# One transfer for each store, and a plan that overlaps operations of ScalarE and VectorE

## The chip, the cores and the metric

The kernel runs on one core of one Trainium2 chip. A core has a matrix engine (TensorE, PE in the profile; PEld is its weight load), a vector engine (VectorE, DVE), a scalar engine (ScalarE, ACT), GpSimd (POOL) and SyncE (SP), which here does nothing but issue transfers. Each engine works through its own list of instructions and waits on semaphores for the others. Sixteen DMA engines move data between DRAM and the on-chip memory. The metric is the time of the whole program on the device, in microseconds; smaller is better.

## The reference

Two mixers over a sequence of S = 2048 positions and D = 640 channels, and a gate that blends them:

```python
kv = k_shift * v                       # k_shift: 4-tap causal shift convolution of k
y  = irfft(rfft(kv) * rfft(ssm_k))     # causal convolution of length 2048 per channel
a  = q * (y + kv * ssm_D)
b  = attention(q @ wqkv) @ wo          # 32 heads of 20, window of 8 keys, dilation 2
g  = sigmoid((q * gate_w).sum(-1, keepdims=True))
out = g * a + (1 - g) * b              # [1, 2048, 640] bf16
```

Here q is `A_q`, which is also the input of the attention.

## The kernel before

**The plan.** The kernel is written as some 25 generators (`vproj`, `score_gen`, `u_stream`, `mults`, ...). Each yields a request `Req`: which engine, a cost in ns, which events must have happened, how many PSUM slots it takes (there are four) or gives back. `Plan.run` keeps, for every engine, the time `self.at[e]` at which it is free, takes in turn the request with the smallest start plus a priority, and lets the generator emit its instructions. So the order of every engine's list, and the choice between ScalarE ("A") and VectorE ("D") where a request allows both ("AD"), follow from these modelled times. On the chip the lists run in that order, and semaphores alone decide when.

**The stages.** `transposes` brings `A_q` into `xT`; `qkproj` (L596) and `vproj` (L534) project; `score_gen` (L662), exponentials (L670) and `pv_gen` (L696) do the attention; VectorE does the shift convolution beside it (L474, L489, L491). The long convolution is a two-step transform: first-stage units of 8 matmuls (`s1_unit`, L729) and second-stage units of 32 (`s2_unit`, L747), first for the filter (`h_stream`), then for kv (`u_stream`), in five groups of 16 channels; each unit's PSUM result is cast by ScalarE (L271) or VectorE (L273). VectorE multiplies the transforms group by group (`mults`, L866 and L869: eight instructions of 128 x 1024 a group). `inverse1` (L883, four units a group) and `inverse2` (L960) go back; `outproj` (L999) makes the attention's output, scaled by 1 - g (L1010) and reordered by GpSimd's transfers into `bl` (L1019).

**The end of the kernel.** `load_q` fetches `A_q` again into `qg`, which takes over the buffer of `kv` (tag "kv"), in 16 transfers of 160 KB; `qscale` (L937, 16 instructions) multiplies `qg` by the gate. For every group of three columns t, `inverse2` makes y in PSUM, ScalarE copies it (L969), VectorE multiplies it into `qg` (L972). `adds` (L1027) adds `bl` to two columns t - 1 and t at a time, and calls `store(t)`.

**The rows.** Partition 32 gg + i of `qg` holds, at column t, the output row 64 i + 16 gg + t. So a pair of columns is, per partition, 2 x 640 values that lie next to each other in the output (2560 bytes), with a step of 64 rows between partitions of a group gg and of 16 rows between the four groups. Before, `store` issues one transfer per group gg, of 32 partitions; for t = 1 and 5 it stores nothing, and at t = 3 and 7 four columns at once. That makes 24 transfers: 20 from SyncE, two from GpSimd (t = 3), two from ScalarE (t = 15).

The load is planned so (L915): a request to GpSimd waits for the last first-stage matmul on kv, and the requests to SyncE that follow it name no event:

```python
yield Req("G", 1.0, [ev("us1")])
...
r = yield Req("S", 900.0, move=us(327680, 1280) * 1.5)
```

Of the kernel before, what the change touches and what calls it, by code (L numbers as in the profile page):

```python
# [18 lines left out]
D = 640  # L19
# [123 lines left out]
LAT = {("P", "A"): 230.0, ("P", "D"): 230.0, ("A", "P"): 120.0, ("D", "P"): 120.0, ("A", "D"): 100.0, ("D", "A"): 100.0}  # L143


MODE = dict(score_gen=1, h_stream=2, u_stream=2, inverse2=4)


class Plan:
# [45 lines left out]
    def best(self, r, name=""):  # L195
        if r.engs == "P":
            st = self.start(r, "P")
            if st == INF:
                return INF, INF, "P"
            st += 110.0 if MODE.get(name) != self.mode else 0.0  # L200
            return self.fetch(st, self.cost(r, "P") * (2.0 if st < 7500.0 else 1.0), r.ins), st, "P"
        return min((self.start(r, e) + self.cost(r, e) + (r.lean if e == "A" else 0.0), self.start(r, e), e) for e in r.engs)

    def run(self):
        while self.streams:
            pick = None
            for k, (pri, gen, r) in enumerate(self.streams):
                end, st, e = self.best(r, gen.__name__)
                if st == INF:
                    continue  # L210
                p = pri if r.pri is None else r.pri
                key = (st + 120.0 * p, p, k)
                if pick is None or key < pick[0]:
                    pick = (key, k, st, end, e)
            assert pick is not None, [s[2].engs for s in self.streams]
            _, k, st, end, e = pick
            pri, gen, r = self.streams[k]
            end -= r.lean if e == "A" else 0.0
            g = Grant()
            g.eng, g.banks = e, []  # L220
            if e == "P":
                self.mode = MODE.get(gen.__name__)
                self.fetch(st, end - st, r.ins, True)
            g.done = Ev(end, e)
            self.at[e] = end
            if r.move:
                at = max(self.pipe, st + 1300.0)
                self.pipe = at + r.move
                g.done = Ev(self.pipe + 700.0, "X")
                self.lane[e].append(g.done.t)  # L230
            if r.take:
                for s in sorted(self.slots, key=lambda s: INF if s.free.t is None else s.free.t)[:r.take]:
                    s.free = Ev(None)
                    g.banks.append(self.slots.index(s))
            for s in r.give:
                self.slots[s].free = Ev(end, e)
            try:
                self.streams[k][2] = gen.send(g)
            except StopIteration:
                del self.streams[k]  # L240
# [3 lines left out]
def kernel(  # L244
# [14 lines left out]
    nc = tc.nc  # L259
# [6 lines left out]
    def raw(ap, off, dims):  # L266
        return bass.AP(tensor=ap.tensor, offset=ap.offset + off, ap=dims)
# [77 lines left out]
    def us(nbytes, run):  # L345
        return 1.1 * nbytes / 16.0 / run * (10.0 + run / 24.0)
# [3 lines left out]
    def loads():  # L350
        def load(name, dst, src, nb, run, deps=()):
            g = yield Req("S", 300.0 + nb / run * 0.5, deps, move=us(nb, run))
            nc.sync.dma_start(dst, src)
            mark(name, g)
# [71 lines left out]
    st = {}  # L426
# [550 lines left out]
                mark(f"pr{t}", e)  # L977

    def store(t):
        if t in (1, 5):  # L980
            return
        t0 = t - 3 if t < 8 else t - 1
        for gg in range(4):
            eng = nc.gpsimd if t < 4 and gg % 2 else nc.scalar if t == 15 and gg % 2 else nc.sync
            eng.dma_start(raw(outf, (16 * gg + t0) * D, [[64 * D, 32], [1, (t - t0 + 1) * D]]),
                          st["qg"][32 * gg:32 * gg + 32, t0:t + 1, :].rearrange("p t c -> p (t c)"))

    def outproj():
        yield Req("G", 1.0, [ev("oT"), ev("wo"), ev("gate")])
# [33 lines left out]
    def adds():  # L1023
        for t in range(1, 16, 2):
            yield Req("D", 740.0, [ev(f"bl{t}"), ev(f"pr{t}")])
            qg, bl = st["qg"], st["bl"]
            nc.vector.tensor_tensor(qg[:, t - 1:t + 1, :], qg[:, t - 1:t + 1, :], bl[:, t - 1:t + 1, :], ALU.add)  # L1027
            store(t)
# [68 lines left out]
```

## Time and profile before

| | before |
|---|---|
| time, median of 3 runs | 251.08 us (249.28 to 254.05) |
| profiled execution: span | 248.4 us |
| TensorE busy | 211.4 us, 85% |
| VectorE busy | 178.4 us, 72% |
| ScalarE busy | 182.5 us, 73% |
| GpSimd busy | 67.7 us, 27% |
| moved by DMA | 42.67 MB, 172 GB/s on average |
| stores of the output to landing | 1.8 us (80 KB), 2.7 us (160 KB) from SyncE |

A busy share is an average over stages that have different limits, so it doesn't tell what a change in one stage is worth. The stages are read from tables of windows, and the order of events in one stage from the timeline. The time to landing of a transfer runs from its issue until its data are there. The profile's span leaves out a small part of the device time.

### The profile page before, as it was taken

How to read it: one execution, taken by the hardware profiler on the slowest of the kernel's cores; microseconds unless marked ns; L12 is line 12 of the kernel's file. 1: busy time of each engine (PE TensorE's matmuls, PEld its weight loads, DVE VectorE, ACT ScalarE, POOL GpSimd, SP SyncE). 2: the span in 40 equal slices, each digit the busy share in tenths (PEclk: the TensorE clock that was granted, in tenths of full speed). 3: DMA queues.
4: the chain of work that ended last, by engine and by line, in shares of the span. 5: the costliest groups of instructions: out<-in, count | busy, mean ns of one | idle time of the engine just before them, and what ended most of it. 6: DMA issues, size and time to landing. Idle time of an engine off the chain costs nothing.

```text
span 248.4 us, 9692 instructions
## 1 busy us (share of the span) xinstructions
PE 211.4 (85%) x4294; PEld 160.9 (65%) x4294; DVE 178.4 (72%) x225; ACT 182.5 (73%) x218; POOL 67.7 (27%) x137
## 2 busy tenths in 40 slices
PE   7999989999999998888889569899979999995400
PEld 3765635655455666566769468889969999994300
DVE  0666879999999644578687667979597639946850
ACT  3437587767787799989998656689797978986810
POOL 7803703664251246340000000033030333033100
PEclk9999999999999999955556979999999999999555
DMA  6997499966697373898994856791140119951464
GB/s 185 354 338 272 114 312 349 280 145 180 109 184 156 96 185 83 196 233 152 284 326 86 197 109 149 159 217 58 57 172 3 55 40 227 205 121 55 137 175 116
DMA packets 51753, 42.67 MB, mean 172 GB/s; under 512 B 27280, under 2 KB 46864, under 8 KB 51712
## 3 DMA queue, kind: packets, MB, share of 16 engines
q1 hardware_dynamic: 46928, 32.87, 52.1%
q0 software_dynamic: 4688, 9.03, 14.1%
q8 instruction: 33, 0.54, 1.0%
q10 hardware_dynamic: 96, 0.16, 0.3%
q14 instruction: 8, 0.07, 0.1%
HBM read 23.51 MB, written 5.25 MB: 116 GB/s over the span
## 4 chain that ended last, share of the span: by engine, by line
PE 49%; DVE 18%; ACT 10%; issue 8%; DMA 7%; SPq 2%; POOL 1%; DVEq 0%; ACTq 0%
PE pj L596 11%; PE op L999 7%; PE i L883 7%; PE psv L534 6%; ACT ET L670 6%; PE s L747 5%; PE O L696 4%; DVE pb L474 4%; DVE pa L489 3%; PE s L729 3%; PE sc L662 3%; DMA qg<-in_A_q_dram 2%; DMA Wv<-in_B_wqkv_dram 2%; DVE Hb L273 2%; SPq L923 2%
## 5 line engine op out<-in xcount | busy, mean ns | idle before, releaser
L670 ACT ACTIVATE ET<-sc 128x726 bf16<-128x726 f32 (+1 forms) x80 | 64.5, 864 | 5.1 <-PE sc L662 4.7
L596 PE MATMUL pj<-xT,Wqk 128*128 128x363 bf16 (+3 forms) x250 | 48.4, 343 | 1.8 <-DVE oS L710 1.2
L596 PEld LDWEIGHTS <-Wqk 128*128 128x128 bf16 x250 | 23.0, 97 | 20.5 <-DVE oS L710 1.9
L747 PE MATMUL s<-Am,Gs 64*128 64x64 bf16 x1280 | 29.7, 201 | 6.4 <-issue 4.1
L747 PEld LDWEIGHTS <-Gs 64*128 64x128 bf16 x1280 | 26.5, 102 | 10.2 <-issue 9.0
L273 DVE CAST Am<-s 128x1024 bf16<-128x1024 f32 x20 | 23.9, 1219 | 6.3 <-PE s L729 6.3
L534 PE MATMUL psv<-Wv,xT 128*128 128x320 bf16 x170 | 25.2, 299 | 1.1 <-DMA Wv<-in_B_wqkv_dram 0.5
L999 PE MATMUL op<-wo,Hb 128*128 128x320 bf16 x160 | 25.1, 304 | 0.0
L883 PE MATMUL i<-M,X 128*128 128x128 bf16 x160 | 21.3, 227 | 0.5 <-DVE X L869 0.5
L271 ACT CAST Am<-s 128x1024 bf16<-128x1024 f32 x20 | 20.0, 1030 | 2.4 <-PE s L729 2.2
L271 ACT CAST X<-i 128x1024 bf16<-128x1024 f32 x19 | 19.1, 1012 | 3.4 <-PE i L883 2.3
L1019 POOL DMA_DIRECT2D bl<-X x12 | 6.3, 532 | 56.0 <-ACT X L1010 56.0
L999 PEld LDWEIGHTS <-Hb 128*128 128x128 bf16 x160 | 20.8, 146 | 0.7
L883 PEld LDWEIGHTS <-X 128*128 128x128 bf16 x160 | 20.4, 149 | 0.9 <-DVE X L869 0.9
L534 PEld LDWEIGHTS <-xT 128*128 128x128 bf16 x170 | 16.0, 98 | 7.6 <-issue 1.0
L662 PE MATMUL sc<-qb,kb 31*128 31x121 bf16 x544 | 18.6, 245 | 2.3 <-DVE oS L710 1.0
L1019 POOL DMA_DIRECT2D bl<-room x20 | 10.4, 526 | 33.9 <-ACT room L1010 33.9
L696 PEld LDWEIGHTS <-ET 128*128 128x128 bf16 x544 | 16.1, 100 | 5.1 <-issue 2.7
L696 PE MATMUL O<-VW,ET 128*128 128x21 bf16 x544 | 16.6, 176 | 2.5 <-ACT ET L670 1.5
L662 PEld LDWEIGHTS <-kb 31*128 31x128 bf16 x544 | 10.3, 103 | 12.1 <-issue 8.5
L489 DVE TENSOR_TENSOR pa<-pa,pb 128x2560 bf16<-128x2560 bf16 x12 | 17.9, 1489 | 0.3
L883 PE MATMUL i<-M,Hs 128*128 128x128 bf16 x128 | 17.1, 228 | 0.4 <-ACT X L271 0.4
(83 smaller groups left out, 380.1 us busy)
## 6 DMA issues: line engine op xcount, KB each, us to landing
X<-Hs SPq DMA_DIRECT2D x16, 256.0 KB, 5.6
Hb<-in_A_k_dram SPq DMA_DIRECT2D x4, 640.0 KB, 10.7
kv<-in_A_v_dram SPq DMA_DIRECT2D x4, 640.0 KB, 12.2
kv_scr<-Hb SPq DMA_DIRECT2D x8, 320.0 KB, 5.2
Hb<-in_A_ssm_k_dram SPq DMA_DIRECT2D x16, 160.0 KB, 5.3
kv<-kv_scr SPq DMA_DIRECT2D x8, 320.0 KB, 5.2
qg<-in_A_q_dram SPq DMA_DIRECT2D x16, 160.0 KB, 6.5
Gs<-cf_G SPq DMA_DIRECT2D x8, 256.0 KB, 7.3
```

Of the source, the lines that this page charges most:

```text
L271: nc.scalar.copy(dst, src)
L273: nc.vector.tensor_copy(dst, src)
L489: nc.vector.tensor_tensor(pa[:], pa[:], pb[:], ALU.add)
L534: nc.tensor.matmul(ps[:, bb, 0:320], lhsT=xT[:, dt, BP * (b0 + bb):BP * (b0 + bb) + 128], rhs=Wv[:, dt, c0:c0 + 320], start=(dt == 0), sto ...
L596: nc.tensor.matmul(ps[:, i, 0:n], lhsT=Wqk[:, dt, w, 128 * ft:128 * ft + 128], rhs=rhs, start=(dt == 0), stop=(dt == NDT - 1))
L662: nc.tensor.matmul(scs[h4 // 2][:, h4 % 2, BP * bb:BP * bb + BP], lhsT=kb[r:r + DH + NF, 128 * b:128 * b + 128], rhs=qb[r:r + DH + NF, BP ...
L670: nc.scalar.activation(ETs[e][:, :, 0:nw], scs[hf][:, :, 0:nw], ACT.Exp, scale=SCALE)
L696: nc.tensor.matmul(O[:, o0:o0 + 21], lhsT=ET[:, hh, BP * bb:BP * bb + 128], rhs=VW[:, b, 4 * t + h4, :], start=True, stop=True, skip_group ...
L747: nc.tensor.matmul(o, lhsT=G[rows, j, rr, :], rhs=Am[rows, 2 * j + rr, :, :], start=(rr == 0), stop=(rr == 1), tile_position=(64 * c, 0), ...
L883: nc.tensor.matmul(o, lhsT=src[:, c, :, :, 8 * oc + il].rearrange("p q j -> p (q j)"), rhs=M[:, k, :], start=(k == 0), stop=(k == 1), skip ...
L999: nc.tensor.matmul(op[:, k, 0:320], lhsT=raw(a, HS * (t % 2) + t // 2, [a.ap[0], [8, 128]]), rhs=wo[:, ft, 320 * k:320 * k + 320], start=( ...
L1019: nc.gpsimd.dma_start(bl[32 * gg:32 * gg + 32, t - 1:t + 1, :].rearrange("p t c -> p (t c)"), raw(row, 0, [[4 * pitch, 32], [1, 1280]]))
```

## The change

Two edits. A store becomes one transfer of all 128 partitions, issued by SyncE, every second column: eight transfers of 320 KB. The four groups gg are now the outermost dimension of the pattern on the side of the DRAM (4 x 32 x 1280). And the plan frees ScalarE 130 ns and VectorE 60 ns before the modelled end of an operation (if it is longer than twice that), since the next operation on these engines starts before the last one has ended. It is for better modelled times, and through them for another order of instructions and another choice between the two engines; it adds and removes no computation.

```diff
+HEAD = dict(A=130.0, D=60.0)
...
             g.done = Ev(end, e)
             self.at[e] = end
+            if end - st > 2.0 * HEAD.get(e, 0.0):
+                self.at[e] -= HEAD.get(e, 0.0)
...
     def store(t):
-        if t in (1, 5):
-            return
-        t0 = t - 3 if t < 8 else t - 1
-        for gg in range(4):
-            eng = nc.gpsimd if t < 4 and gg % 2 else nc.scalar if t == 15 and gg % 2 else nc.sync
-            eng.dma_start(raw(outf, (16 * gg + t0) * D, [[64 * D, 32], [1, (t - t0 + 1) * D]]),
-                          st["qg"][32 * gg:32 * gg + 32, t0:t + 1, :].rearrange("p t c -> p (t c)"))
+        t0 = t - 1
+        nc.sync.dma_start(raw(outf, t0 * D, [[16 * D, 4], [64 * D, 32], [1, (t - t0 + 1) * D]]),
+                          st["qg"][:, t0:t + 1, :].rearrange("p t c -> p (t c)"))
```

In the built program, seen engine by engine, the plan's new times move many instructions. TensorE, VectorE, ScalarE and GpSimd keep their work but for the stores and a few casts: net, five casts of 1024 columns go from VectorE to ScalarE. In VectorE's list the 16 `qscale` instructions stood behind the multiplications of all five groups; in the changed list they stand behind those of the third group, ahead of the last two. Of the 16 output projections ten stood ahead of the last first-stage matmul on kv in TensorE's list, and now eight do.

## The prediction

> **What bounds the kernel now.** I read the share of each engine by stage first, then the timeline of the last 50 us, then the waits of SyncE. The stages (columns: stretch in us, its length, busy us and count of PE, PEld, DVE, ACT, POOL, granted clock, DMA share, GB/s):
>
> ```profile
> 150.00:180.00 30.00, 28.94 (x707) 26.91 (x705) 22.94 (x25) 22.95 (x24) 4.22 (x8) 1.00 0.55 125
> ...
> 203.36:221.97 18.61, 18.26 (x352) 17.18 (x350) 15.06 (x30) 15.91 (x18) 5.43 (x11) 1.00 0.94 196
> 221.97:239.43 17.46, 7.68 (x522) 5.97 (x522) 14.36 (x26) 11.16 (x14) 3.11 (x6) 0.76 0.41 117
> 239.43:248.40 8.97, 0.00 (x0) 0.00 (x0) 0.00 (x1) 0.00 (x0) 0.00 (x0) 0.50 0.45 109
> ```
>
> Up to 221.97 TensorE is the bound (97 to 98% busy), then VectorE (82%), and for the last 8.97 us no engine computes: only stores run. The timeline around the load of `qg`, and then at the end (start, length, engine, line, operation, out<-in, and in brackets the idle time before it and what ended that):
>
> ```profile
> 202.81 0.51 PE L729 MATMUL s<-F1b,kv 64*128 64x128 bf16 x8
> ...
> 203.36 10.22 SPq L923 DMA_DIRECT2D qg<-in_A_q_dram  x16
> ...
> 205.29 0.68 DVE L866 TENSOR_TENSOR Hs<-X,Hs 128x1024 bf16<-128x1024 bf16 x1
> ```
>
> ```profile
> 220.63 0.39 DVE L937 TENSOR_SCALAR qg<-qg,g_nat 128x640 bf16<-128x640 bf16 x1 [3.26 <-issue]
> ...
> 221.32 2.16 DVE L937 TENSOR_SCALAR qg<-qg,g_nat 128x640 bf16<-128x640 bf16 x7 [0.29 <-DMA qg<-in_A_q_dram]
> ...
> 221.90 1.02 PE L960 MATMUL i<-X,T 32*32 32x160 bf16 x96
> ...
> 229.30 16.02 SPq L985 DMA_DIRECT2D out_dram<-qg  x20
> ...
> 237.88 1.55 DVE L1027 TENSOR_TENSOR qg<-qg,bl 128x1280 bf16<-128x1280 bf16 x2
> ```
>
> Two things are to be seen. The load of `qg` begins when the last first-stage matmul on `kv` (L729) ends, because it takes that buffer, and its last piece is there only at 221.32, 17.96 us later. VectorE waits for it 3.26 us, but all its multiplications (L866, L869) are behind it by then, and TensorE never notices. And the last add ends at 239.43, while SyncE is still issuing stores until 245.32, about 0.45 us each, after a pause in its wait list:
>
> ```profile
> SPq L985 <- DMA out_dram<-qg: 2.4, 1, 2.4
> ```
>
> **What the Trainium skill says.** (1) "DMA: Bandwidth & Descriptors", section "Why a DMA increments its semaphore by 16 and not by 1": a transfer is spread over k of the 16 engines, the largest k up to 16 that divides the size of the slowest dimension, not 1, of both access patterns. No transfer of SyncE in the trace of before has such a dimension under 16, so it neither agrees nor disagrees. (2) The same page, "Issuing engines are not separate DMA queues": issuing from several engines saves issue time alone. The trace fits: an 80 KB store takes 1.8 us to landing from SyncE and from ScalarE alike. (3) "Perfetto Trace Analysis", "Tensor Engine Instruction": VectorE and ScalarE take their instructions strictly in order. The wait of 3.26 us above, with nothing passing it, agrees. (4) "TensorE: Matmul & The Clock Gate", Part 1: after some 3.4 us of idleness the clock halves. The trace agrees: 32 L747 matmuls take 1.03 us at 113.25 (stage at 0.74) and 0.57 at 202.41 (stage at 1.00).
>
> **The change part by part.**
>
> *Fewer stores.* 24 transfers of 80 or 160 KB (20 from SyncE, 2 from GpSimd, 2 from ScalarE) become 8 of 320 KB from SyncE. Issue falls from 20 x 0.45 us to 8 x 0.45, so the issue queue behind the last add goes away. If each store ran on 16 engines, the end would be: 0.1 us wait, 1.6 us fixed (the 1.8 us to landing less 0.2 us of moving), the last two stores' data (0.9 us each at the rate below), and the 1.7 us that lie now between the last landing (244.89 + 1.8) and 248.4: 5.2 us instead of 8.97, a gain of 3.8.
>
> *The shape of a store.* The new DRAM pattern is 4 x 32 x 1280, so by (1) k is 4: each of four engines carries 327,680 / 4 = 81,920 B per store, and all eight stores want the same four. The rate of one engine I take from the transfers of SyncE in 124 to 130 us, most of them with the same rows of 2560 B; the other two lines bound it: the stores themselves at 242.5 to 245, and long rows at 18 to 24. Columns: packets, MB, share of 16 engines.
>
> ```profile
> q1 hardware_dynamic: 1175, 2.03, 94.9%
> ```
>
> ```profile
> q1 hardware_dynamic: 259, 0.44, 73.3%
> ```
>
> ```profile
> q1 hardware_dynamic: 618, 1.63, 71.7%
> ```
>
> 2.03 MB / (0.949 x 16 x 6 us) = 22.3 GB/s; the stores give 0.44 / (0.733 x 16 x 2.5) = 15.0, the long rows 1.63 / (0.717 x 16 x 6) = 23.7. So a store takes 3.7 us (3.5 to 5.5), eight 29.4 us (27.7 to 43.7). The adds that release them follow each other within some 13 us, so the stores queue and the end is first add + 0.1 + 1.6 + 29.4 + 1.7 = first add + 32.8.
>
> *The plan.* HEAD lets the planner start the next ScalarE or VectorE operation 130 or 60 ns early. That is about what the trace shows (ScalarE casts of 1.01 us start 0.9 apart, L866/L869 of 0.68 start 0.60 apart), but costs nothing itself: it only moves work. In the built order five casts of 1024 columns, net, go over from VectorE to ScalarE; up to the last L729 TensorE's work differs by two output projections only (of 16, ten stood ahead of that matmul, now eight). The earlier stages I book at nothing, within 3 us either way: TensorE has the same instructions and is the bound there, and the row of casts beside it has room (ScalarE 77 to 86% busy in 150 to 203).
>
> What I do book is VectorE's tail. In the built order of before the 16 `qscale` instructions (L937) stand behind all multiplications. In the changed order they stand **ahead of the multiplications of the last two groups**. The planner believes `qg` to be there earlier than it is: `load_q` waits for the last L729 with a GpSimd request, but its eight SyncE requests carry no dependency. Queued behind the first waiting `qscale`: 8 multiplications of group 3, a cast, 8 of group 4. Waiting for those: ScalarE's evictions of group 4 (they overwrite what the multiplications read), so all four PSUM slots, so TensorE, which runs dry about 5 us after the last L729. From that matmul's end, t0:
> - t0: 203.35 less two output projections of 1.4 us = 200.5.
> - `qg` landed: 17.96, less the 8 of 12 `bl` transfers that can't run in the jam. GpSimd's queue took 19.2% of the engines over 19 us for 12, so 8 are 2.4 us: t0 + 15.5.
> - the last seven `qscale`, 0.3 each: 17.7. Multiplications of group 3, 8 x 0.60: 22.5.
> - TensorE: four inverse units (L883) at 1.0 and two projections at 1.4, 0.2 of wait: 29.5. Its clock will be down; half speed for some 4 us costs 2: 31.5.
> - s2 unit 0.6, wait 0.2, VectorE's cast 1.2: 33.5. Multiplications of group 4: 38.3. (Four projections, 5.6 us, lie beside them.)
> - four inverse units and a wait 4.3, last eviction 1.4: 44.0.
>
> So the second inverse (L960) starts at 244.5 instead of 221.97, 22.5 us later. The first add ends 4.4 us after that start (221.97 to 226.37 now): 248.9.
>
> *Sum.* 248.9 + 32.8 = 281.7 us of span against 248.4: +33.3. With 251.08 us before: **284.4**.
>
> **The rivals.**
> - *Jam, but stores on all engines.* For it: nothing in this trace shows a narrow transfer. Last add at 244.5 + 17.5 - 1.5 (no projection lies between any more) = 260.5, + 5.2 = 265.7; +17.3: 268.4.
> - *Narrow stores, no jam.* For it: the 3.26 us wait cost nothing before. Against: the order. 226.4 + 32.8 = 259.2; +10.8: 261.9.
> - *Neither, faster than before.* The issue queue shrinks as meant, 3.8 us: 247.3. Against it stand both arguments.
> - *Slower stores still*, at 15.0 GB/s: +14.3 on the forecast, 298.7. It's the top of the forecast's own case.
>
> **How the numbers follow.** The forecast's case 0.82; it spans 277 (clock penalty 2.0, rate 1.7 and earlier stages 3 us better) to 299 (the slow rate); jam alone 0.09, narrow stores alone 0.05, neither 0.04. Of the first I leave out the top; with the second that makes 8 in 10 for 267 to 297. Faster by over 2% is half of the last case, within 2% the other half and a little.
>
> **What would show it.** Right: VectorE idle 12 us or more ahead of L937, TensorE idle beside it; L866 of group 3 only after L937; stores landing 5 us after issue and later ones 15 to 20; the last landing 20 us or more behind the last add; a DMA share near 0.25 with all four engines busy. Wrong: DMA share over 0.5 while stores run alone (k is 16), or the second inverse starting before 230 (no jam).

## The result, and the profile after

| | before | after |
|---|---|---|
| time, median of 4 runs | 251.87 us (249.28 to 254.05) | 282.97 us (281.35 to 286.37) |
| ratio to before, 95% interval | | 1.125 (1.110 to 1.140) |
| profiled execution: span | 248.4 us | 281.4 us |
| TensorE / VectorE / ScalarE busy | 211.4 / 178.4 / 182.5 us | 215.8 / 171.5 / 185.7 us |
| granted clock of TensorE, mean | 0.896 | 0.845 |

Here and below the medians are of all runs, while the ratios compare only the fast ones, since some executions of one and the same kernel take 1.5 to 3% longer than its others.

The engines do almost the same work, and most of the 33.0 us that the span has grown by are waiting. (In the traces six casts of 128 x 1024, net, have moved from VectorE to ScalarE, 39 and 66 before and 33 and 72 after, where the built order had been read as five.) Two stretches hold the waiting. Both are in the windows of the changed kernel (columns as before: stretch in us, its length, busy us and count of PE, PEld, DVE, ACT, POOL, granted clock, DMA share, GB/s):

```profile
200.00:205.00 5.00, 4.24 (x84) 3.72 (x84) 0.00 (x0) 1.12 (x2) 1.68 (x4) 1.00 1.06 219
205.00:210.00 5.00, 0.00 (x0) 0.00 (x0) 0.39 (x1) 0.00 (x0) 0.00 (x0) 0.79 1.09 196
210.00:215.00 5.00, 0.00 (x0) 0.00 (x0) 2.16 (x7) 0.00 (x0) 0.00 (x0) 0.50 0.98 174
215.00:220.00 5.00, 0.00 (x0) 0.00 (x0) 4.25 (x11) 0.11 (x1) 0.00 (x0) 0.50 0.01 2
220.00:225.00 5.00, 3.19 (x50) 2.85 (x50) 3.12 (x6) 4.11 (x5) 1.50 (x3) 0.50 0.05 18
225.00:230.00 5.00, 5.00 (x44) 4.27 (x43) 0.00 (x0) 2.82 (x3) 0.58 (x2) 0.66 0.13 49
...
260.00:265.00 5.00, 0.00 (x0) 0.00 (x0) 0.00 (x0) 0.00 (x0) 0.00 (x0) 0.50 0.26 102
265.00:270.00 5.00, 0.00 (x0) 0.00 (x0) 0.00 (x0) 0.00 (x0) 0.00 (x0) 0.50 0.26 104
270.00:275.00 5.00, 0.00 (x0) 0.00 (x0) 0.00 (x0) 0.00 (x0) 0.00 (x0) 0.50 0.26 103
```

From 205 to 220 TensorE and ScalarE, which before were busy for 14.65 and 13.23 us of these 15, do next to nothing; until 215 the DMA engines are full (shares of 0.98 to 1.09), and from then to 220 VectorE works almost alone. From 260 on nothing computes and the share of the DMA engines stands at 0.26, steady to the last digit: of 16 engines, four. The records of the single packets (a packet is one row of 2560 bytes) say so too: from 260 to 270 four of them are under way at 87% of the time and five at the rest, never fewer and never more. The timeline says who waits. VectorE's, and then SyncE's (start, length, engine, line, operation, out<-in, and in brackets the idle time before it and what ended that):

```profile
208.60 0.39 DVE L942 TENSOR_SCALAR qg<-qg,g_nat 128x640 bf16<-128x640 bf16 x1 [11.19 <-DMA qg<-in_A_q_dram]
210.38 2.16 DVE L942 TENSOR_SCALAR qg<-qg,g_nat 128x640 bf16<-128x640 bf16 x7 [1.39 <-DMA qg<-in_A_q_dram]
215.60 2.70 DVE L942 TENSOR_SCALAR qg<-qg,g_nat 128x640 bf16<-128x640 bf16 x8 [3.07 <-DMA qg<-in_A_q_dram]
218.22 0.68 DVE L871 TENSOR_TENSOR Hs<-X,Hs 128x1024 bf16<-128x1024 bf16 x1
...
247.96 0.82 DVE L1028 TENSOR_TENSOR qg<-qg,bl 128x1280 bf16<-128x1280 bf16 x1
...
258.35 1.55 DVE L1028 TENSOR_TENSOR qg<-qg,bl 128x1280 bf16<-128x1280 bf16 x2
```

```profile
198.97 11.54 SPq L928 DMA_DIRECT2D qg<-in_A_q_dram  x16
248.81 16.03 SPq L986 DMA_DIRECT2D out_dram<-qg  x8
```

And TensorE's last work before the gap, its first after it, and the start of the second inverse (L965 here):

```profile
202.92 1.58 PE L1000 MATMUL op<-wo,Hb 128*128 128x320 bf16 x10
220.96 1.04 PE L752 MATMUL s<-Am,Gs 64*128 64x64 bf16 x32 [16.46 <-ACT X L276]
...
244.32 1.87 PE L965 MATMUL i<-X,T 32*32 32x160 bf16 x192 [1.10 <-ACT X L276]
```

Lines have moved by one to five against the kernel before: L942 is `qscale`, L871 and L874 the multiplications, L1028 the adds, L986 the store, L752 and L276 second-stage units and their ScalarE casts. Before, `qscale` waited 3.26 us when all multiplications were done. Now it waits 11.19 + 1.39 + 3.07 us, and the multiplications of two groups can only run after it. The list of waits (engine, line, waited for: us in total, times, longest) shows the same wait three times, handed on from engine to engine:

```profile
ACT X L276 <- DVE X L874: 18.8, 1, 18.8
PE s L752 <- ACT X L276: 16.5, 1, 16.5
...
DVE qg L942 <- DMA qg<-in_A_q_dram: 15.7, 3, 11.2
```

The last add ends at 259.90; the span ends 21.5 us later. Before, this rest was 8.97 us.

### The profile page after: what moved, and what is told of

It reads as the page before. It is cut to its first block, busy times and chain, and to the rows that moved or that the text cites. A ratio compares the mean times of both kernels' runs of the same rounds, so it can differ in the third digit from the quotient of the medians.

```text
span 281.4 us, 9680 instructions
## 1 busy us (share of the span) xinstructions
PE 215.8 (77%) x4294; PEld 164.5 (58%) x4294; DVE 171.5 (61%) x221; ACT 185.7 (66%) x222; POOL 67.0 (24%) x135
## 4 chain that ended last, share of the span: by engine, by line
PE 41%; DVE 13%; ACT 12%; DMA 12%; issue 9%; POOL 3%; SPq 2%; DVEq 0%; ACTq 0%; POOLq 0%
PE pj L601 9%; PE i L888 7%; PE op L1000 6%; DMA qg<-in_A_q_dram 5%; PE s L752 4%; PE O L701 4%; ACT ET L675 3%; PE psv L539 3%; ACT Am L276 3%; PE sc L667 3%; ACT X L276 2%; DMA kb<-Gs 2%; PE s L734 2%; DMA Wv<-in_B_wqkv_dram 2%; POOL kb L637 2%
## 5 line engine op out<-in xcount | busy, mean ns | idle before, releaser
L675 ACT ACTIVATE ET<-sc 128x726 bf16<-128x726 f32 (+1 forms) x80 | 63.8, 862 | 4.5 <-PE sc L667 3.9
L752 PE MATMUL s<-Am,Gs 64*128 64x64 bf16 x1280 | 29.2, 199 | 21.2 <-ACT X L276 16.5
L752 PEld LDWEIGHTS <-Gs 64*128 64x128 bf16 x1280 | 26.1, 101 | 23.1 <-issue 21.7
L278 DVE CAST Am<-s 128x1024 bf16<-128x1024 f32 x22 | 26.3, 1219 | 10.5 <-PE s L734 10.5
L276 ACT CAST X<-s 128x1024 bf16<-128x1024 f32 x17 | 17.1, 1026 | 19.8 <-DVE X L874 18.8
L888 PE MATMUL i<-M,X 128*128 128x128 bf16 x160 | 22.6, 236 | 0.6 <-DVE X L874 0.6
L276 ACT CAST X<-i 128x1024 bf16<-128x1024 f32 x20 | 20.1, 1018 | 3.1 <-PE i L888 3.1
L667 PE MATMUL sc<-qb,kb 31*128 31x121 bf16 x544 | 18.0, 243 | 2.6 <-DMA kb<-sH 0.8
L637 POOL DMA_DIRECT2D qb<-Gs x21 | 11.5, 553 | 33.2 <-ACT Gs L276 11.6
L888 PE MATMUL i<-M,Hs 128*128 128x128 bf16 x128 | 18.7, 238 | 0.6 <-DVE Hs L871 0.6
L276 ACT CAST Am<-s 128x1024 bf16<-128x1024 f32 x18 | 18.0, 1032 | 0.4 <-PE s L734 0.4
```

The costliest lines, as they stand in the source:

```text
L276: nc.scalar.copy(dst, src)
L278: nc.vector.tensor_copy(dst, src)
L637: nc.gpsimd.dma_start(dst[r0:r0 + fb - fa, 0:wd], stg[fa - f0:fb - f0, 0:wd])
L667: nc.tensor.matmul(scs[h4 // 2][:, h4 % 2, BP * bb:BP * bb + BP], lhsT=kb[r:r + DH + NF, 128 * b:128 * b + 128], rhs=qb[r:r + DH + NF, BP ...
L675: nc.scalar.activation(ETs[e][:, :, 0:nw], scs[hf][:, :, 0:nw], ACT.Exp, scale=SCALE)
L752: nc.tensor.matmul(o, lhsT=G[rows, j, rr, :], rhs=Am[rows, 2 * j + rr, :, :], start=(rr == 0), stop=(rr == 1), tile_position=(64 * c, 0), ...
```

## The experiments

Ten kernels, each the kernel before or the changed one with one or two parts exchanged.

### The plan without the new stores

```diff
 # the changed kernel
     def store(t):
-        t0 = t - 1
-        nc.sync.dma_start(raw(outf, t0 * D, [[16 * D, 4], [64 * D, 32], ...
+        # as in the kernel before: one transfer for each row group
```

> The changed kernel with the stores of before. Theory (four engines carry the new stores, the order of VectorE's list makes the rest): VectorE's wait ahead of L942 and the start of the second inverse stay as in the changed kernel (some 15 us idle, start at 244), the end is again the last add + about 9 us, as before: 270 us. Rival A (the order alone makes the loss, the width of a store is of no account): no gain, or slower by the longer issue queue, 283 to 287. Rival B (the stores alone): 252.

Measured: 271.39 us beside 250.78 for before; ratio 1.081 (1.073 to 1.088). The jam is there unchanged; VectorE's timeline of this kernel:

```profile
210.51 0.39 DVE L942 TENSOR_SCALAR qg<-qg,g_nat 128x640 bf16<-128x640 bf16 x1 [11.09 <-DMA qg<-in_A_q_dram]
212.50 2.16 DVE L942 TENSOR_SCALAR qg<-qg,g_nat 128x640 bf16<-128x640 bf16 x7 [1.60 <-DMA qg<-in_A_q_dram]
217.67 2.65 DVE L942 TENSOR_SCALAR qg<-qg,g_nat 128x640 bf16<-128x640 bf16 x8 [3.02 <-DMA qg<-in_A_q_dram]
```

The last add ends at 260.34 and the span 9.0 us later, the rest that the kernel before has. So the plan alone costs 20.6 us, all of it ahead of the last add.

### The new stores without the plan

```diff
 # the kernel before
     def store(t):
-        ... one transfer for each row group
+        t0 = t - 1
+        nc.sync.dma_start(raw(outf, t0 * D, [[16 * D, 4], [64 * D, 32], ...
```

> The kernel before with the new stores and nothing else. Theory: first add at 226.4 as before, end 33 us later, share of the DMA engines about 0.25 while stores alone run: 262 us. Rival A (width of no account, fewer issues help): 247 to 248.

Measured: 262.6 us; ratio 1.047 (1.039 to 1.055), so the stores alone cost 11.8 us. Now nothing jams (the second inverse starts at 221.54), and the windows of this kernel show the four engines by themselves:

```profile
240.00:250.00 10.00, 0.00 (x0) 0.00 (x0) 0.00 (x0) 0.00 (x0) 0.00 (x0) 0.50 0.26 103
```

Both parts together, 20.6 + 11.8 = 32.4 us, are close to the 31.1 us of the change: the two costs add, since the adds that release the stores come later by the jam and the stores take as long afterwards.

### `qscale` behind the multiplications

```diff
 # the changed kernel, in qscale
-            r = yield Req("D", 230.0, [ev(f"qg{t // 8}"), ev("gate")])
+            r = yield Req("D", 230.0, [ev(f"qg{t // 8}"), ev("gate"), ev("mult4")])
```

The added event is in the planner's model only. In the traces it moves the 16 instructions behind all multiplications; with them the planner gives one cast of 1024 columns back to VectorE and places some output projections earlier.

> The changed kernel with one edit of the plan: the 16 qscale instructions are also made to wait for the last multiplication, so they stand behind all multiplications in VectorE's list. Theory: no stall of VectorE and TensorE, second inverse starts at about 220, the stores still take 33 us from the first add to the end: 260 to 262 us. Rival A (order alone): 249 to 251. Rival C (other moves of the plan in the earlier stages cost): 268 or more, with the last first-stage matmul on kv later than 203.

Measured: 262.84 us; ratio 1.046 (1.039 to 1.053). The load was requested at 199.36, within 0.4 us of the changed kernel, and VectorE still waits ahead of the second half of `qscale`, but now for 4.46 us and with no multiplication behind it. (The profile names no releaser for this wait; that it is the load is read from the eight instructions that it stands before.) VectorE's line, and TensorE's first of the second inverse:

```profile
218.84 2.66 DVE L942 TENSOR_SCALAR qg<-qg,g_nat 128x640 bf16<-128x640 bf16 x8 [4.46 <-issue]
```

```profile
220.65 1.02 PE L965 MATMUL i<-X,T 32*32 32x160 bf16 x96 [1.10 <-ACT X L276]
```

The second inverse starts at 220.65 instead of 244.32. So the jam goes with the place of these 16 instructions. The plan's moves that both kernels share don't make it; the one cast of 1.2 us and the output projections that moved along weren't tried apart, but it is the wait ahead of `qscale`, with the multiplications behind it, that the changed kernel's trace shows.

With the old stores as well, the plan is left alone and freed of the jam:

```diff
 # the changed kernel
+            ... ev("mult4") in qscale, as above
+        ... stores as in the kernel before
```

> The changed plan with the stores of before and qscale behind all multiplications: what is left of HEAD is the other order in the earlier stages. Theory: the last first-stage matmul on kv ends at 199 instead of 203.4, but two output projections more (2.8 us) follow it, so the second inverse starts about 1.5 us earlier: 249 to 251 us. Rival C (the plan's other moves cost something): 253 or more.

Measured: 248.15 us; ratio 0.988 (0.982 to 0.993). The plan's new times bring 1.2% in this measurement, a little more than expected: the last first-stage matmul on `kv` comes some 4 us sooner (load requested at 199.00 instead of 203.36), and 2.0 us of it reach the last add (237.40 instead of 239.43).

### Telling the planner what the load waits for

```diff
 # the changed kernel with the old stores, in load_q
-                r = yield Req("S", 900.0, move=us(327680, 1280) * 1.5)
+                r = yield Req("S", 900.0, [ev("us1")], move=us(327680, 1280) * 1.5)
```

> The changed plan with the stores of before, and the planner told what holds the load of qg: its eight SyncE requests name the last first-stage matmul on kv. Theory (the planner put qscale too early because it thought qg was there): qscale goes behind all multiplications by itself, and the time is that of the run with qscale placed by hand, 247 to 250 us. Rival: qscale stays ahead, 270.

Measured: 249.0 us; ratio 0.995 (0.991 to 0.998), with nothing said about `qscale`. The planner puts it behind the multiplications by itself; VectorE's timeline has the first eight at 211.95 without a wait, and the others after the last multiplication:

```profile
218.69 0.39 DVE L942 TENSOR_SCALAR qg<-qg,g_nat 128x640 bf16<-128x640 bf16 x1 [4.28 <-issue]
```

By the traces, every engine's list is the same, instruction for instruction, as in the kernel with `ev("mult4")` and the old stores. So 248.15 and 249.0 us (0.988 and 0.995 of the kernel before, each on its own chip) are two measurements of one program: what the plan gains without the jam is 0.5 to 1.2%, and a difference of this size between kernels that were measured apart says little.

So in this kernel a change of 60 and 130 ns in the model became 20 us through a wait that the buffer enforces and the plan didn't know. Whether the kernel before, told the same, would change too wasn't tried.

### Two engines instead of four

Each pair of columns in two transfers of 64 rows, outermost size 2:

```diff
 # the kernel before
+        for hf in range(2):
+            nc.sync.dma_start(raw(outf, (32 * hf + t0) * D, [[16 * D, 2], [64 * D, 32], ...
```

> The kernel before with each store cut into two transfers of 64 rows, each with the row groups outermost in the DRAM pattern (2 x 32 x 1280). Theory (the outermost size is the number of engines): two engines carry everything, share of the DMA engines about 0.13 while stores alone run, 2.62 MB over two engines at 25 GB/s are 52 us, the end at 226.4 + 57: 285 to 289 us. Rival D (a store is slow because 128 rows are one transfer or because the pattern has three dimensions, on whatever engines): no slower than one transfer, 258 to 264.

Measured in one run: 287.22 us. The same bytes in twice as many transfers take far longer, and the windows say why:

```profile
250.00:275.00 25.00, 0.00 (x0) 0.00 (x0) 0.00 (x0) 0.00 (x0) 0.00 (x0) 0.50 0.13 52
```

Share and rate are half of the four-engine stores' 0.26 and 103 GB/s: 0.13 x 16 is two engines. So it isn't the size of a transfer, nor the step of 16 rows, but the outermost size of the pattern that sets how many engines serve it. Here the outermost sizes are 2, 4 and 32, and the engines follow: two (two packets under way at 93% of the time from 250 to 275, three at the rest), four, and with the 32 rows of one group a share of up to 1.02 in the last adds' stretch of the kernel before. A transfer of all 128 rows with a large outermost size wasn't tried.

### More issuing engines for the old stores

Could a different split gain what the change was meant to gain, the queue of issues behind the last add? First with GpSimd taking the odd row groups of every pair:

```diff
 # the kernel before
-            eng = nc.gpsimd if t < 4 and gg % 2 else nc.scalar if t == 15 and gg % 2 else nc.sync
+            eng = nc.gpsimd if gg % 2 else nc.scalar if t == 15 else nc.sync
```

> The kernel before with the issue of its stores shared: the odd row groups from GpSimd, the even ones from SyncE (ScalarE for the last pair), each still a transfer of 32 rows. Theory: the issue queue behind the last add shrinks from 5.9 us to about 1, all 16 engines carry each store: the end 4.5 to 5.5 us after the last add instead of 9.0, 246 to 248 us. Rival: the data or a wait for earlier stores sets the end, not the issue: 250 to 251.

Measured: 257.14 us, ratio 1.024 (1.016 to 1.032): a miss, in the other direction. The windows show that the stores themselves did what was hoped: the rate at the end is up (173 and 177 GB/s in these first two windows before) and all data are out by 246.

```profile
242.00:244.00 2.00, 0.00 (x0) 0.00 (x0) 0.00 (x0) 0.00 (x0) 1.40 (x3) 0.50 0.90 279
244.00:246.00 2.00, 0.00 (x0) 0.00 (x0) 0.00 (x0) 0.00 (x0) 0.00 (x0) 0.50 0.38 142
246.00:248.00 2.00, 0.00 (x0) 0.00 (x0) 0.00 (x0) 0.00 (x0) 0.00 (x0) 0.50 0.00 0
```

But the span ends at 254.5. What runs until then is GpSimd's closing DRAIN, which isn't counted as busy and appears only when the program's last line is queried (count, shortest/median/longest in ns, first and last start). First this kernel, then the kernel before:

```profile
L1092 POOLq DRAIN  x3: 46/108/10936, 242.8 to 254.3; - x3
```

```profile
L1092 POOLq DRAIN  x3: 46/242/10072, 230.1 to 248.1; - x3
```

In these two kernels it takes 10 to 11 us from GpSimd's last request on. Before, that request was at 230 and the drain lay beside the last adds and stores. At 243 it becomes the end of the program. The same split on the freed plan behaves the same way:

> The changed plan with qscale behind all multiplications, and the shared issue of stores. Theory: both gains add up, 248.2 less 3 to 4.5 us: 243.5 to 245.5 us. Rival (the end of this plan is set elsewhere): 247 to 248.

Measured: 252.96 us; ratio 1.007 (1.003 to 1.010), instead of the gain expected. The drain starts at 239.4 and takes 10.9 us; the data are out by 241.5, and the span ends at 251.2.

Then with ScalarE in GpSimd's place, for the last three pairs only:

```diff
 # the kernel before
-            eng = nc.gpsimd if t < 4 and gg % 2 else nc.scalar if t == 15 and gg % 2 else nc.sync
+            eng = nc.gpsimd if t < 4 and gg % 2 else nc.scalar if t >= 11 and gg % 2 else nc.sync
```

> The kernel before, with one edit: the stores of the odd row groups of the last three pairs are requested by ScalarE in place of SyncE (GpSimd takes only those of the pairs below four, so its last transfer stays where it was, near 230 us). Own theory: after the last addition the program waits for a row of about 0.4 us issues on SyncE and then the landing; with half of them on ScalarE the row is done 2 to 3 us earlier and GpSimd's closing drain, over by about 241, stays hidden: 247 to 249 us. Rival: ScalarE's issues stand before its last casts and hold up VectorE's last addition, or the transfers are limited by the engines and not by the issues: 250 to 252 us, no difference.

Measured: 250.46 us; ratio 1.000 (0.997 to 1.004), as the rival had it. ScalarE's timeline and VectorE's:

```profile
236.38 0.92 ACTq L985 DMA_DIRECT2D out_dram<-qg  x2
237.40 1.62 ACT L969 CAST X<-i 128x960 bf16<-128x960 f32 x3 [2.68 <-DMA out_dram<-qg]
```

```profile
238.39 1.13 DVE L972 TENSOR_TENSOR qg<-X,qg 128x960 bf16<-128x960 bf16 x3 [1.47 <-ACT X L969]
239.44 1.55 DVE L1027 TENSOR_TENSOR qg<-qg,bl 128x1280 bf16<-128x1280 bf16 x2
```

ScalarE's first two issues, for the pair of t = 10 and 11, stand ahead of its last three casts and hold them up 2.68 us; VectorE waits 1.47 us for these. The last add ends at 240.99 instead of 239.43 and the rest after it falls from 8.97 to 6.9 us: what the shorter queue brings, the later add gives back. Together with the told load:

> The changed kernel with the plan of both queues' costs, the old stores, the load of the second operand told its wait (as in s6_load_told), and the same sharing of the last stores with ScalarE as in s10_act_shares. Own theory: the two gains add, 249 less 2 to 3: 245 to 247.5 us, faster than every kernel run so far. Rival: no gain from the sharing, 248 to 250 us.

Measured: 248.9 us; ratio 0.990 (0.987 to 0.993). Again the last add comes later (239.54, against 237.63 in the kernel with the told load and the old stores) and the rest is shorter (6.8 us, against 9.0), so hardly more is left than without the sharing. The new plan without the jam, with the old stores (0.988 and 0.995) or with this sharing of them (0.990), can't be ranked by these intervals; each measurement is faster than the kernel before, by 0.5 to 1.2%, and than the changed one, by about 12%.

## Why the prediction was right

It said 284.4 us, and 282.97 were measured. By its own steps, in the trace of the changed kernel:

| step | predicted | measured |
|---|---|---|
| t0, end of the last first-stage matmul on `kv` | 200.5 | 198.97 |
| `qg` landed | t0 + 15.5 | t0 + 16.6 (second half of `qscale` at 215.60) |
| VectorE idle ahead of L942 | 12 us or more | 15.7 us |
| multiplications of group 3 end | t0 + 22.5 = 223.0 | 223.1 |
| four inverse units, two projections, cold clock | 31.5 - 22.5 = 9.0 us | 9.2 us, clock 0.50 to 0.66 |
| second inverse starts | 244.5 | 244.32 |
| first add ends | 248.9 | 248.78 |
| first add to the end | 32.8 us | 32.6 us |
| span | 281.7 | 281.4 |

- **The jam** was right in cause and order: the two kernels with `ev("mult4")` and the one with the told load are without it, and the kernel with the old stores has it alone. The fall-off of the clock, booked at 2 us, was needed: TensorE came back at half clock after some 16 us of idleness, and its first projection then took 2.46 us where the next took 1.53. But the lines that the prediction gave for it don't show that idleness halves the clock: around 113.25 TensorE was 26.03 of 30 us busy (105 to 135 of the kernel before), at a clock of 0.50 for a reason that no run here shows. The changed kernel does show it: TensorE ends at 204.50, and a mean of 0.79 from 205 to 210 between the two states 1.00 and 0.50 puts the fall some 2.9 us into that window, 3.4 us after the last matmul.
- **The stores** were right in the number of engines, which no line of the trace before could show. The Trainium skill's rule ("DMA: Bandwidth & Descriptors", section "Why a DMA increments its semaphore by 16 and not by 1") is what carried it, and here the traces agree twice, at outermost sizes of 4 and 2.
- **The rivals' prices** hold as well: the stores alone were put at 261.9 and gave 262.6; the jam with stores on all engines at 268.4. The kernel nearest to it, with the old stores, keeps the queue of issues that this rival had taken away at 3.8 us: 268.4 + 3.8 = 272.2, and it gave 271.4.

That the span came within 0.3 us is luck: several terms were off and cancelled. t0 came 1.5 us earlier, a gain in the stages ahead of it, which were booked at nothing, within 3 us; the load of `qg` was 1.3 us shorter than before (17.96 to 16.6) and not 2.4 as booked for the `bl` transfers left out; eight `qscale` instructions and not seven ran after it had landed (2.70 us); and one DMA engine moved 103 / (0.26 x 16) = 25 GB/s and not 22.3. At 103 GB/s eight stores of 327,680 bytes take 25.5 us instead of 29.4. The difference went into a slow beginning: from the end of the first add to that of the last the stores moved 60 GB/s on average, not 103, which the prediction, taking them as one unbroken queue, didn't have. Why they are slower there (84 GB/s from 253 to 256, 76 from 256 to 260) stays open. The four engines are busy all the time, but some thirty packets of a row take 0.18 to 1.15 us each, where later ones take 0.10. VectorE at work isn't enough to explain it: with the new stores alone it is busy from 235 to 239 without a break, and the stores move 104 GB/s. Open too is why the new stores cost 14.7 us on the freed plan (262.84 - 248.15) and 11.8 on the plan before; the traces put most of it into the time from the first add to the end, 34.5 us beside 32.4.

## What to carry to other kernels

Where engines run their lists in order, an instruction that waits for a load is priced by what stands behind it, so read the built order of the waiting engine before the sizes of the costs; and give a planner every wait that the hardware will enforce, buffer reuse included, or a change of 60 ns in its model can put the wait in front of the bound. When transfers are merged to save issues, look at the outermost size of the merged pattern: a small one there can take most of the DMA engines away, and the DMA share of a stretch in which transfers run alone tells it at once. And count GpSimd's closing drain before giving it a late transfer.

## What the hardware showed that was not expected

- GpSimd's closing drain takes 10.1 to 10.9 us with the old stores (10,072 ns in the kernel before, 10,936 ns with the late stores), beginning with its last transfer, and ends the program if that transfer comes late: 254.5 us of span with all data out by 246. It isn't a constant: in three kernels where stores on two or four engines ran beside it (the new stores alone, two halves, `qscale` behind the multiplications) it takes 12.8 to 13.2 us, and GpSimd's last data are out only some 8 us after it began. What it waits for stays open. The Trainium skill's "DMA: Bandwidth & Descriptors", section "Issuing engines are not separate DMA queues", says that another issuing engine saves issue time alone; the measurement adds what it can cost.
- An issue can be held up by the transfers before it: in the changed kernel SyncE's eight issues of stores take 537 to 4356 ns (median 636), where the 20 before took 314 to 1007 ns (median 396). It is not the shape alone, since the first five take at most 0.69 us each. With two halves, six in a row from 249 on take 2.97 to 3.11 us each, about the 3.2 us in which one store of 163,840 bytes moves at 52 GB/s.
